# A linear-attention and bilinear-FFN kernel on one core: when chunk 1's inputs are loaded, and the orders of chunks 0 to 2

## The chip, the core and the metric

The kernel runs on one core of a Trainium2 chip. The time is the device time of one execution in microseconds (us); with one core, the slowest core is that core. A few executions are timed, and the median is given. One further execution is profiled; its span (first to last instruction) is a little shorter than its time.

The engines of the core work side by side, each through its own queue in order: TensorE (PE; its weight loads are listed as PEld), VectorE (DVE), ScalarE (ACT), GpSimd (POOL) and SyncE (SP, which here only issues transfers).

## The reference

Two stages, one after the other. First a recurrent linear attention with a gate per row of the state, for 4 batch rows, 8 heads, 768 steps and head size 48:

```python
for t in range(S):
    state = alpha[:, :, t, :, None] * state + np.einsum('bhd,bhe->bhde', k[:, :, t], v[:, :, t])
    y[:, :, t] = np.einsum('bhd,bhde->bhe', q[:, :, t], state)
```

Then a feed-forward layer on the 3,072 tokens of 384 features, with 1,536 hidden columns:

```python
a = x @ w_a
b = x @ w_b
return (a * b @ w_out).astype(np.float32)
```

All inputs and the output are float32. The kernel casts the weights and most operands of its matmuls to bf16.

## The kernel before

**Tiling.** The 768 steps are cut in three blocks of 256, and the batch in two pairs of rows: six chunks, numbered 0 to 5. Chunks 0 and 1 are the first 256 steps of rows 0 and 1, and of rows 2 and 3; the state is zero there. The 256 steps of a chunk lie on 128 partitions as pairs of consecutive steps. A chunk has two batch rows, called u = 0 and 1 below, and 512 tokens for the feed-forward layer.

**Stages of a chunk.** Load alpha, k, q, v (`ld`, L411); logarithm of alpha on ScalarE (`ln`, L418); prefix sums of the logarithms by matmuls with a triangular matrix (`B` L460, `A2` L510, `AQ` L505, with the even half's subtraction `Bs` L465 in chunk 0); exponentials of the sums, with both signs (`E`, L539); products of q and k with these (`mq`, `mk`, L550), for the first step of each pair also with alpha or its inverse (`lv`, L524); transposes by TensorE into PSUM and copies out of it (`C` L591, `Ce` L597 or L599), or by DMA in later chunks (`T`, L602); scores (`D`, L672), their causal mask (`M` on VectorE, L677; or `Mc` on ScalarE, L681, and `Mm` in place on VectorE, L685); state products (`K`, `KA`, L625) and the two state updates (`k`, L657, L660, L661), with decays from TensorE (`dk` L571, `de` L576) or by way of DRAM (`dr` L556, `dl` L561); the products of queries with carried states (`SA`, `SB`, L696 or L701) and of masked scores with v (`Y`, L696 or L722); the eviction of the result as xT (`X`, L762 or L764).

Then the feed-forward layer: hidden columns go in 12 blocks of 128. Block f of the gate (`a`) and of the up product (`b`) are three matmuls each (L784), over 512 tokens or, for one u alone, over 256. The gate is copied out by ScalarE (`as`, L790), and VectorE multiplies copy and up product (`pr`, L798). Output rows are four tiles of 128 tokens per chunk, each 12 matmuls in two halves (`o`, L806), evicted (`ot`, L821 or L823) and stored (`st`, L839).

**Weights.** `W a` and `W b` load columns of the two hidden weights and `Wo` blocks of the output weights, all issued by GpSimd (L391, L394). Each comes in pieces: columns 0 to 256, 256 to 768, 768 to 1,536.

**What sets the order.** The kernel is written with a manual schedule. A string, `PROGRAM` (L17 to L265), lists the operations chunk by chunk in one sequence, and a loop at the end (L927) records them in that order. Each engine then works through its own operations in the string's order, and waits only where data or a buffer are not ready; an operation of one engine that stands late in the string does not hold up another engine's. So a transfer is issued by its queue's engine (P is GpSimd, Y is SyncE, V VectorE, S ScalarE) after that engine's operations that stand ahead of it in the string. PSUM has 8 banks; the last number of many operations is the bank that they take, and a bank is free again once its reader is done. One buffer for v as bf16 (`vx`), two for the scaled q and k (`QKp`), and three for the gate copies (`as_`) are shared by the chunks.

The constants are part of the string: `c1`, `cz`, `cs` clear tiles, `fill` runs matmuls on zeros, `cm 0` and `cm 1` make the two halves of the mask on GpSimd (L363 to L367), `c2`, `c3` cast the triangular matrix (L354, L357).

In the first 60 us the string of before issues on GpSimd, after chunk 0's second-row inputs: the first up weights, the mask's second half, v, the casts, the first gate weights, chunk 1's alpha of row 1, the gate and up weights to 768, chunk 1's alpha of row 0, the gate and up weights to 1,536, then chunk 1's q and k, the output weights between the inputs of chunks 1 and 2, and so on.

Of the kernel before, what the change touches and what calls it, by code (L numbers as in the profile page):

```python
# [26 lines left out]
1: ld q 0 P; ln 1  # L27
0: b 0 0 4; a 0 0 2; as 0 0; pr 0 0; D 1 0 6; D 1 1 0; M 1 1
1: ld k 0 P; l2 1 P; ld v 0 P; ld k 1 P
0: Mc 1 0; Mm 1 0 V  # L30
1: H 1 S
0: SB 1 1; a 2 0 3; a 5 0 6; a 3 0 7; as 3 0; a 4 0 4; as 4 0; as 5 0; b 4 0 0; b 3 0 7
1: L 1 V
0: pr 4 0; pr 3 0; SA 1; Y 1; X 1 V; b 2 0 0
1: A2 1 7; ld q 1 P
0: Wo 0 6
2: ld a * P
0: K 1 1 5
# [36 lines left out]
1: Y 0; D 1 1 0; SA 0; X 0 S; Mc 1 1
0: o 3 1 -; ot 3 S
1: a 2 0 4
0: o 0 1 -
1: as 2 0; b 2 0 5
2: lx V; R 0; R 1; ra 1; lv 1 q P  # L80
3: ld q * P
2: AQ 3; E 0 b; E 1 b
0: ot 0 S
2: E 1 i; E 0 i
1: D 1 0 1; pr 2 0; M 1 0; a 11 0 0
0: o 1 0 7
2: ra 0
1: as 11 0
2: dr; dl
1: Mm 1 1 V; v 1 V  # L90
0: st 3 Y; o 1 1 -; ot 1 V
1: a 7 0 3; b 11 0 1; pr 11 0; KA 1 64; k 1 0 V; k 1 1 V; b 10 0 5; a 10 0 7; as 10 0; a 0 0 6
2: lv 0 k V
1: pr 10 0; b 0 0 1; a 3 0 4; as 0 0; pr 0 0
# [36 lines left out]
1: o 2 1 -; ot 2 S
0: st 2 Y
1: st 2 Y
2: D 0 0 5; Mc 0 0; Mm 0 0 V; SB 0 1; SA 1; Y 1; X 1 S; XT 1
1: a 4 1 7
4: ln *
1: as 4 1; b 9 1 0; pr 9 1; o 0 0 5
3: AQ 3
2: SA 0; Y 0; X 0 S; XT 0
5: ld a * Y  # L140
1: o 0 1 -; ot 0 V; a 1 1 6; a 10 1 1; as 1 1; as 10 1
3: E 0 b; E 0 i
1: b 4 1 2; pr 4 1; b 8 1 5; b 1 1 1; a 8 1 6; b 10 1 0; pr 1 1; o 3 0 2; pr 10 1; as 8 1; pr 8 1; o 3 1 -; ot 3 S; st 3 Y
2: a 4 * 7; as 4 *
3: E 1 b
2: a 5 * 6; b 4 * 3
3: E 1 i
1: st 0 Y
3: dr
4: lx V; R 0  # L150
3: mk 0 V; mq 0 V; T 0
4: ld q * Y
2: a 1 * 2; b 5 * 0; as 5 *; pr 5 *
4: ra 1
2: b 7 * 4; b 10 * 1; pr 4 *; a 10 * 6; as 10 *; pr 10 *
# [12 lines left out]
2: a 11 * 5; as 11 *; pr 11 *
1: o 1 1 -; ot 1 S
2: a 6 * 5; as 6 *; a 8 * 3; as 8 *  # L170
3: SB 0 6; D 0 1 0; M 0 1; T 1
4: ld k * Y
3: D 1 0 4; Mc 1 0
2: b 6 * 2; pr 6 *; b 8 * 3; pr 8 *
4: R 1
3: Mm 1 0 V
4: lv 1 q V
3: SB 1 4; D 1 1 0; Mc 1 1; Mm 1 1 V; SA 0; Y 0; X 0 S; XT 0
2: o 0 0 2
4: lv 1 k V; lv 0 k V  # L180
2: o 0 1 -
4: AQ 6; E 0 i
2: ot 0 S
4: E 0 b
3: SA 1; Y 1; X 1 V; XT 1
5: ld k * Y
4: E 1 i; E 1 b; mk 1 V
5: lv 1 k P
2: o 2 0 1; o 2 1 -; o 3 0 6; o 1 0 0; o 3 1 -; o 1 1 -
4: dr  # L190
1: st 1 Y
3: a 11 * 5
2: ot 2 V; ot 3 V
# [29 lines left out]
3: pr 10 *
4: SA 1; SA 0; Y 0; X 0 S; XT 0
3: o 2 0 7; o 1 0 1
4: Mm 1 0 V
# [28 lines left out]
4: ot 1 V; o 3 0 1; o 3 1 -; ot 3 V; o 0 0 4; o 0 1 -
3: st 3 Y
5: a 3 * 7; as 3 *; b 0 * 1; b 3 * 3; a 0 * 5; as 0 *; pr 0 *; pr 3 *
# [705 lines left out]
```

## Time and profile before

| | |
|---|---|
| timed runs, median of 3 | 196.4 us (195.39 to 196.49) |
| profiled execution, time | 195.32 us |
| profiled execution, span | 193.5 us |
| bytes read from HBM, written | 25.98 MB, 4.74 MB |
| VectorE, ScalarE, GpSimd busy | 138.4, 103.3, 50.8 us |

On the page, TensorE's busy time counts modelled ends of pipelined matmuls, so neighbours overlap: the distance from the start of a group to the start of the next tells what it costs. The costliest groups are the gate and up matmuls (L784), 57.0 and 56.1 us, and the output matmuls (L806), 48.5 us. In the timelines a row is a group of equal instructions: start, time from its start to its last end, engine, line, operation, what it writes and reads, sizes, count, and in brackets the idle time of the engine before it with what ended that. In the chain of waits a row has start and length, and the engine and line that the end of the program hung on in that stretch.

### The profile page before, as it was taken

The numbers are of one execution on the slowest core, as the hardware profiler recorded it, in microseconds if no ns is written. First come the engines' busy times: TensorE is split into PE (matmuls) and PEld (weight loads), VectorE is DVE, ScalarE is ACT, GpSimd is POOL, SyncE is SP. The second block draws the span as 40 slices with busy tenths as digits, with TensorE's granted clock in tenths as the row PEclk, the third lists the DMA queues.
The fourth block names the chain that finished last, engine by engine and source line by source line (L and its number), as shares of the span: only waits on it lengthen the run. The fifth ranks groups of instructions, "written<-read, shape, count | busy, mean of one in ns | idle before, by whom it ended". The sixth has DMA issues, their size and how long they took to land.

```text
span 193.5 us, 5877 instructions
## 1 busy us (share of the span) xinstructions
PE 184.7 (95%) x2509; PEld 111.4 (58%) x2509; DVE 138.4 (71%) x230; ACT 103.3 (53%) x189; POOL 50.8 (26%) x71
## 2 busy tenths in 40 slices
PE   7889699999999998999999999999999999999993
PEld 3467475666687865744556644555544566544462
DVE  4688777999899799597979499875854871156520
ACT  4565575886775676556565235875255622154401
POOL 8999645850640425000400020050000000000000
PEclk9999999999999999999999999999999999999999
DMA  5999999999999999489995488999297005021013
GB/s 139 261 214 211 243 247 251 252 246 260 243 220 231 198 234 219 57 233 213 172 219 69 100 203 178 118 191 120 59 180 160 3 3 122 0 99 67 0 42 122
DMA packets 67162, 30.96 MB, mean 160 GB/s; under 512 B 58064, under 2 KB 65120, under 8 KB 67136
## 3 DMA queue, kind: packets, MB, share of 16 engines
q0 software_dynamic: 18640, 14.16, 41.3%
q1 hardware_dynamic: 48352, 16.34, 39.9%
q8 instruction: 19, 0.31, 0.7%
q10 hardware_dynamic: 144, 0.10, 0.2%
q14 instruction: 7, 0.06, 0.1%
HBM read 25.98 MB, written 4.74 MB: 159 GB/s over the span
## 4 chain that ended last, share of the span: by engine, by line
PE 84%; POOL 6%; DMA 5%; issue 2%; DVE 1%; ACT 0%; POOLq 0%; DVEq 0%
PE psum L784 47%; PE psum L806 24%; DMA wb_t<-in_moe_w_b_dram 5%; PE psum L672 3%; PE psum L722 2%; PE psum L625 2%; PE psum L696 2%; PE psum L701 1%; PE psum L505 1%; PE psum L817 1%; POOL v_t L411 1%; POOL a_t L411 1%; PE psum L591 1%; POOL wa_t L391 1%; DVE prod L798 1%
## 5 line engine op out<-in xcount | busy, mean ns | idle before, releaser
L784 PE MATMUL psum<-xT,wb_t 128*128 128x512 bf16 (+1 forms) x270 | 57.0, 337 | 1.3 <-DMA wb_t<-in_moe_w_b_dram 1.3
L784 PE MATMUL psum<-xT,wa_t 128*128 128x512 bf16 (+1 forms) x270 | 56.1, 337 | 0.0
L806 PE MATMUL psum<-wo_t,prod 128*128 128x384 bf16 x276 | 48.5, 326 | 0.0
L784 PEld LDWEIGHTS <-wb_t 128*128 128x128 bf16 x270 | 25.5, 98 | 21.9 <-DMA wb_t<-in_moe_w_b_dram 1.6
L784 PEld LDWEIGHTS <-wa_t 128*128 128x128 bf16 x270 | 25.6, 98 | 19.7 <-issue 0.2
L806 PEld LDWEIGHTS <-prod 128*128 128x128 bf16 x276 | 26.1, 98 | 17.0
L681 ACT ACTIVATE m<-psum 128x1024 bf16<-128x1024 f32 x16 | 16.3, 1023 | 6.1 <-PE psum L672 5.9
L823 DVE COPY ot<-psum 128x384 f32<-128x384 f32 (+1 forms) x13 | 6.9, 538 | 15.7 <-PE psum L806 13.2
L524 POOL TENSOR_TENSOR q_t<-q_t,ra 128x384 f32<-128x384 f32 x8 | 8.8, 1103 | 34.7 <-DVE prod L798 18.4
L821 ACT ACTIVATE ot<-psum 128x384 f32<-128x384 f32 (+1 forms) x12 | 5.7, 477 | 12.9 <-PE psum L806 11.9
L524 POOL TENSOR_TENSOR k_t<-k_t,a_t 128x384 f32<-128x384 f32 x5 | 6.0, 1197 | 22.8 <-DVE QKp L550 17.9
L685 DVE TENSOR_TENSOR m<-m,mask 128x1024 bf16<-128x1024 bf16 x16 | 11.6, 734 | 0.3 <-ACT m L681 0.2
L418 ACT ACTIVATE la<-a_t 128x1536 f32<-128x1536 f32 (+2 forms) x9 | 9.5, 1053 | 3.7 <-DMA a_t<-in_alpha_dram 3.7
L550 DVE TENSOR_TENSOR QKp<-k_t,invb 128x768 bf16<-128x768 f32 x10 | 11.0, 1105 | 0.2
L677 DVE TENSOR_TENSOR m<-psum,mask 128x1024 bf16<-128x1024 f32 x8 | 9.8, 1219 | 1.6 <-PE psum L672 1.5
L550 DVE TENSOR_TENSOR QKp<-q_t,beta 128x768 bf16<-128x768 f32 x10 | 9.3, 947 | 0.0
L672 PE MATMUL psum<-kqT 64*64 64x128 bf16 x384 | 8.6, 218 | 0.2 <-DVE kqT L599 0.2
L411 POOL DMA_DIRECT2D v_t<-in_v_dram x8 | 8.6, 1075 | 0.6 <-PE psum L784 0.5
L762 ACT ACTIVATE ys<-psum 128x768 bf16<-128x768 f32 x7 | 5.6, 808 | 5.6 <-PE psum L722 3.3
L672 PEld LDWEIGHTS <-kqT 64*64 64x64 bf16 x384 | 6.3, 107 | 2.7 <-issue 2.3
L411 POOL DMA_DIRECT2D a_t<-in_alpha_dram x6 | 6.3, 1043 | 5.6 <-DVE prod L798 2.9
L444 PE MATMUL psum<-wz 128*128 128x512 bf16 x17 | 5.5, 473 | 1.2 <-DVE og L336 1.2
(272 smaller groups left out, 272.0 us busy)
## 6 DMA issues: line engine op xcount, KB each, us to landing
out_dram<-ot SPq DMA_DIRECT2D x23, 192.0 KB, 2.6
a_t<-in_alpha_dram POOLq DMA_DIRECT2D x3, 768.0 KB, 14.2
k_t<-in_k_dram SPq DMA_DIRECT2D x3, 768.0 KB, 6.7
q_t<-in_q_dram POOLq DMA_DIRECT2D x2, 768.0 KB, 12.8
v_t<-in_v_dram POOLq DMA_DIRECT2D x4, 384.0 KB, 9.2
q_t<-in_q_dram SPq DMA_DIRECT2D x2, 768.0 KB, 6.7
a_t<-in_alpha_dram POOLq DMA_DIRECT2D x3, 384.0 KB, 5.7
q_t<-in_q_dram POOLq DMA_DIRECT2D x3, 384.0 KB, 13.1
```

Source lines behind the costliest of these rows:

```text
L411: eng.dma_start(out=t[:, us, hs].rearrange("p b h r d -> p (b h) (r d)"), in_=src[ch.b0 + us.start:ch.b0 + us.stop, hs, ch.s * 2 * C:(ch.s ...
L418: nc.scalar.activation(out=ch.la[:, us, hs].rearrange("p b h r d -> p (b h r d)"), in_=ch.a[:, us, hs].rearrange("p b h r d -> p (b h r d) ...
L524: eng.tensor_mul(x, x, by)
L550: eng.tensor_mul(QKp[ch.c % 2][:, u, j, :, hs, :D], src[:, u, hs].rearrange("p h r d -> p r h d"), f)
L672: nc.tensor.matmul(s2[g * HC:(g + 1) * HC, r, p, rk, :], lhsT=ch.kqT[u][rs, 1, rk, 2 * h + p, g * HC:(g + 1) * HC], rhs=queriesT(ch, u, 2 ...
L677: nc.vector.tensor_mul(m.rearrange("p r a k s -> p (r a) (k s)"), ch.s2[u, h].rearrange("p r a k s -> p (r a) (k s)"), maskn(4))
L681: nc.scalar.activation(out=m.rearrange("p r a k s -> p (r a) (k s)"), in_=ch.s2[u, h].rearrange("p r a k s -> p (r a) (k s)"), func=AF.Copy)
L685: eng.tensor_mul(x, x, maskn(4))
L784: nc.tensor.matmul(p, lhsT=(wa_t, wb_t)[w][:, kk, f * 128:(f + 1) * 128], rhs=ch.xT[:, us.start // 2:us.stop // 2, kk].rearrange("p u g s ...
L806: nc.tensor.matmul(op, lhsT=ch.prod[:, f, at:at + C], rhs=wo_t[:, f, :], start=(f == 0), stop=(f == NFF - 1))
L821: nc.scalar.activation(out=o_, in_=i_, func=AF.Copy)
L823: eng.tensor_copy(o_, i_)
```

## The change

Only `PROGRAM` is new. The set of operations is the same but for their engines, buffers and tokens per operation; the functions that they call are the same.

- Loads. Chunk 0's rows come in the same order on SyncE. On GpSimd the first gate weights and both alpha pieces of chunk 1 now stand ahead of the first up weights; the gate and up weights to column 768 follow; then chunk 1's k and q of row 0, q of row 1 and v of row 0, and only then the gate weights from 768, chunk 1's k of row 1, and the up weights from 768. Chunk 2's alpha, chunk 1's v of row 1, chunk 2's q and k, and chunk 3's alpha follow, and after them both halves of the output weights.
- Chunk 0. The product of decays of row 0 stands ahead of the transposes; the second half of the mask is made after the loads down to chunk 1's alpha of row 1; all four score tiles are masked by VectorE out of PSUM (before: two of them by ScalarE's copy and a masking in place). Gate and up products of blocks 0 to 5 run for one row at a time, blocks 6 to 11 for both.
- Chunk 1 runs its gate and up products for one row at a time before chunk 0's output matmuls start, which now follow all but a few of them.
- Three products `lv` go from GpSimd to VectorE, two casts of v from VectorE to ScalarE; one more copy of transposes and one more eviction are VectorE's.
- Chunks 3 to 5 keep TensorE's order.

The start of the string before and after:

```diff
-0: c1a; c1; fill 7 2; cz 0 q V; cz 0 b P; cs 0 m P; ci; cz 1 q V; cz 0 v V; ld a 0b Y; ln 0b; cs 0 0 P; cm 0; cu; cu2 P; B 0b 3; Bs 0b; cs 1 m P; ld v 0 P; ld a 1 P
-0: cz 1 b P; ld a 0a Y; ln 0a; B 0a 1; Bs 0a; E 0a b; fill 9 2; cus; ld q 0a Y; mq 0a V; E 0b i; ld q 0b Y; ld k 0a Y; ld k 0b Y; mk 0b V; E 0b b; mq 0b V
-0: C 0 1 5; E 0a i; mk 0a V; Ce 0 1 V; C 0 0 3; Ce 0 0 V; dk 0 6; fill 1 1; v 0 S; de 0; K 0 0 7; k 0 0 V; ln 1; cs 1 0 P; ld q 1 P; ld k 1 P; W b 0 256
-0: cm 1; ld v 1 P; c2 P; c3 P; D 0 1 5; M 0 1; D 0 0 0; SB 0 6; B 1a 4; Bs 1a; Mc 0 0; Mm 0 0 V; B 1b 5; Bs 1b; E 1a i; E 1a b; mq 1a V; mk 1a V; K 0 1 4; E 1b i
-0: v 1 V; mk 1b V; E 1b b; mq 1b V; SA 0; Y 0; X 0 S; dk 1 0; C 1 0 3; Ce 1 0 V; k 0 1 V; b 1 0 6; W a 0 256; de 1; K 1 0 5; k 1 0 V
-1: ld a 1 P
-0: W a 256 768; W b 256 768
-1: ld a 0 P
-0: W a 768 1536; C 1 1 1; a 1 0 2; as 1 0; pr 1 0; Ce 1 1 V; W b 768 1536
-1: ld q 0 P; ln 1
...
+0: c1a; c1; cz 0 b P; ld a 0b Y; cs 0 m P; fill 7 2; cz 0 q V; ci; ld a 0a Y; cz 1 q V; ld q 0a Y; cs 0 0 P; cz 0 v V; ld q 0b Y; cm 0; ld k 0a Y; ld k 0b Y; ln 0b; cu; ln 0a
+0: cu2 P; cs 1 m P; B 0b 3; ld v 0 P; B 0a 1; Bs 0b; ld a 1 P; fill 9 2; Bs 0a; cus; E 0a b; cz 1 b P; cs 1 0 P; E 0b i; mq 0a V; ld q 1 P; E 0b b; E 0a i; mk 0b V; dk 0 6
+0: c2 P; mq 0b V; c3 P; C 0 1 5; ld k 1 P; mk 0a V; v 0 S; Ce 0 1 V; C 0 0 3; ld v 1 P; de 0; K 0 0 4; Ce 0 0 S; D 0 1 0; k 0 0 V; W a 0 256; fill 1 5; ln 1; SB 0 5
+1: ld a 1 P
+0: D 0 0 2; B 1a 4; cm 1; M 0 1; M 0 0; B 1b 0; Bs 1a; K 0 1 2; Bs 1b; E 1a b
+1: ld a 0 P
+0: SA 0; Y 0; E 1a i; mq 1a V; E 1b i; W b 0 256; mk 1a V; E 1b b; mk 1b V; X 0 S; dk 1 3; W a 256 768; v 1 S; mq 1b V; C 1 0 0; k 0 1 V; C 1 1 5; W b 256 768; de 1; K 1 0 6
+0: Ce 1 1 V
+1: ld k 0 P
+0: Ce 1 0 V
+1: ln 1; ld q 0 P
+0: D 1 1 2; k 1 0 V; M 1 1
+1: ld q 1 P; ln 0
+0: SB 1 0; D 1 0 4; a 0 0 6
+1: l2 1 P
+0: a 1 0 7; M 1 0; as 0 0; b 1 0 3
...
+0: W a 768 1536
+1: H 0 S
+0: pr 0 0; X 1 S
+1: A2 1 7; L 0 V; ld k 1 P
+0: a 1 1 5; pr 1 0
+1: A2 0 1
+0: W b 768 1536; a 2 1 0
...
+0: a 10 * 4; pr 5 1
+1: lv 1 k P
+0: pr 3 1
+1: SB 0 6
+0: as 10 *; a 8 * 3
+3: ld a * P
+1: mk 1 V
+0: as 7 *; a 11 * 4
+1: Mm 0 0 V; C 1 1 1
+0: Wo 6 12; as 11 *
+1: Mm 0 1 V; C 1 0 5; Ce 1 1 S
+0: b 7 * 0; Wo 0 6
...
+2: dl; D 1 0 5; D 1 1 2; KA * 70; Mc 1 0; M 1 1
+0: o 1 1 -
+2: k * 0 V
+0: o 2 0 1; ot 1 S; st 1 Y
+2: D 0 0 4
+0: st 3 Y
+2: D 0 1 2
+4: ld a * Y
+2: M 0 0
+0: o 2 1 -
+2: Mc 0 1; Mm 1 0 V; SB 1 6
+0: ot 2 S
+2: SB 0 2
```

More of the change, by code (lines that the diff above doesn't have):

```diff
@@ L63 @@
+1: mk 0 V
+0: b 0 1 6; a 3 0 0; pr 5 0; a 4 0 4
+1: lv 0 q P
+0: as 3 0; pr 0 1; a 4 1 3; as 5 1; pr 3 0; a 3 1 0; as 4 1
+2: ld q * P
+0: b 4 0 6
+1: mq 0 V
+0: as 4 0; b 4 1 5
+1: E 1 b; C 0 1 1
+0: pr 4 1
+2: ld k * P
+1: C 0 0 4
+0: as 3 1
+1: Ce 0 1 V; v 0 S; dk * 3; Ce 0 0 V; lv 1 q P; D 0 1 1; de *; KA 0 07
+0: pr 4 0
+1: Mc 0 1
+0: K 1 1 5
+1: D 0 0 3; k 0 0 V
+0: k 1 1 V; b 5 1 6
+1: Mc 0 0
+0: b 3 1 0
+1: mq 1 V
+0: a 6 * 2; a 7 * 5
+1: k 0 1 V
+0: a 10 * 4; pr 5 1
 1: lv 1 k P
+0: pr 3 1
@@ new lines @@
+2: lv 1 q P
+1: pr 1 0; a 9 0 1; k 1 0 V; a 0 0 5; pr 2 0; as 9 0
+3: ld q * P
+1: b 0 0 0
+2: R 0; ra 0
+1: as 0 0; SB 1 5; a 6 0 1; b 3 0 2
+2: lv 0 q V; ld v * P
+1: as 6 0; b 6 0 7; pr 0 0; a 3 0 1
+2: R 1
+1: b 9 0 3; as 3 0; Y 1
+3: ln *
+1: pr 9 0; pr 6 0; SA 1
+2: AQ 0
+1: pr 3 0
+2: lv 0 k V
+1: X 1 S
+0: a 9 * 7
+2: E 1 b
+3: lx V
+0: b 9 * 2; as 9 *
+1: a 4 1 5
+2: E 1 i
+1: a 11 1 6; k 1 1 V
+2: E 0 b
+1: a 6 1 7; b 9 1 3
+2: dr
+0: pr 9 *
+1: as 6 1
+2: E 0 i
+1: b 6 1 1; a 9 1 7; as 11 1; pr 6 1; a 3 1 2; as 9 1
@@ L78 @@
+2: mq 1 V
+1: a 5 1 6; as 4 1; b 1 1 7; b 11 1 5; pr 9 1; a 0 1 1; pr 11 1; b 8 1 3; as 0 1
+2: mk 1 V
+1: a 8 1 4; b 0 1 1; as 8 1; a 2 1 5; pr 0 1
+2: T 1
+0: o 3 0 4
+3: R 0
+1: as 5 1; a 1 1 6
+2: mq 0 V
+0: o 3 1 -
+1: pr 8 1; b 2 1 0
+2: mk 0 V
+1: as 3 1; b 5 1 3
+3: ra 0
+0: o 0 0 2; ot 3 S
+3: R 1; lv 0 q P
+2: T 0
+1: b 4 1 4
 0: o 0 1 -
[L79 to L82, printed above, removed]
+1: pr 4 1; pr 5 1; as 2 1
+3: ld k * P
+0: o 1 0 4
+1: as 1 1; pr 2 1
@@ new lines @@
+1: b 3 1 5
+3: lv 0 k P
+1: as 7 1; b 7 1 1; pr 3 1; a 10 1 4
+2: k * 1 V; Y 1
+1: as 10 1
+2: Y 0
+3: ld v * P; lv 1 k V
+2: SA 1; SA 0
+3: AQ 4
+2: X 1 S; X 0 V
+5: ld a * P
+3: ra 1
+1: o 0 0 0
+2: XT 1
+3: E 0 b; E 0 i; mq 0 V
+1: o 2 0 6
+3: E 1 i
+2: XT 0
+4: ln *
+3: lv 1 q V
+1: o 2 1 -
+3: mk 0 V
+1: o 0 1 -
+4: ra 1
+1: b 10 1 7; ot 0 S; o 3 0 2; pr 10 1
+3: E 1 b
+1: st 0 Y; pr 7 1
+3: dr
+1: ot 2 V
+2: a 4 * 3; a 5 * 6; b 4 * 0; as 5 *; a 1 * 5; as 4 *
+1: o 3 1 -
+2: pr 4 *
+3: T 0
@@ L132 @@
+2: b 5 * 3
+1: ot 3 V
+2: b 10 * 0; pr 5 *; b 7 * 1
+4: lx V
+2: a 10 * 6
+0: st 0 Y
+2: a 7 * 3
+1: st 3 Y
+2: as 10 *
 0: st 2 Y
+4: R 0
+2: b 1 * 2; as 1 *
 1: st 2 Y
[L134 to L143, printed above, removed]
@@ L175 @@
+3: M 0 0
+4: lv 0 q P; ld k * Y
+2: b 11 * 0
+4: ld v * P
+3: k * 0 V
+2: a 11 * 5
+1: o 1 1 -
+3: k * 1 V
+2: as 11 *; a 6 * 5
+1: ot 1 S
+2: pr 11 *; a 8 * 3; as 6 *
+3: SB 0 6
+2: as 8 *
+3: D 0 1 0; D 1 0 4; M 0 1
+2: b 6 * 2
+3: Mc 1 0
+2: b 8 * 3; pr 6 *
+3: SB 1 4; D 1 1 0
+2: pr 8 *
+3: SA 0; Y 0; Mc 1 1
 4: R 1
-3: Mm 1 0 V
+2: o 0 0 2
+3: X 0 S; Mm 1 0 V; XT 0
+2: o 0 1 -
 4: lv 1 q V
[L178 to L181, printed above, removed]
@@ L222 @@
+4: D 0 1 5; D 0 0 3; k * 0 V
+3: b 1 * 7
+4: Mc 0 0
+3: a 3 * 0
+5: ld q * Y
+3: pr 1 *
+5: ra 0
+3: b 4 * 3
+4: Mc 0 1
+3: a 2 * 4; pr 4 *
+5: ra 1
+3: b 2 * 7; as 2 *
+4: Mm 0 0 V; gatet 1
+5: ld v * P
+3: a 7 * 1; as 3 *
+4: Mm 0 1 V
+3: a 10 * 2; pr 2 *; as 7 *
+4: SB 0 3; SB 1 5
+3: as 10 *
+4: D 1 1 0
+3: b 3 * 7
+4: Mc 1 1
+3: b 10 * 2; pr 3 *
+4: D 1 0 0; Mm 1 1 V
 5: lv 1 q P
[L223 to L226, printed above, removed]
+4: SA 1; SA 0; Mc 1 0; Y 0
+3: pr 10 *; o 2 0 7
@@ L252 @@
-5: XT 1; X 0 S
+3: o 0 1 -; ot 1 V
+4: a 7 * 0
+5: mk 0 V
+3: ot 0 S
+4: b 1 * 4; as 7 *
+5: mq 1 V
+4: b 7 * 5
+5: mq 0 V
+4: a 10 * 3
+5: T 1
+4: a 1 * 1; as 10 *; a 6 * 6; as 1 *; b 10 * 2
+5: T 0
+4: a 0 * 0; pr 10 *; b 0 * 1; pr 7 *; as 0 *; a 2 * 2; pr 1 *; as 6 *; b 6 * 7; pr 0 *; as 2 *
+5: dl
+4: b 5 * 0; pr 6 *; a 5 * 3
+3: st 1 Y
+4: b 2 * 7
+3: st 2 Y
+4: as 5 *
+3: st 0 Y
+4: a 3 * 5; pr 2 *; a 4 * 2; as 3 *; pr 5 *; a 11 * 7; as 4 *
+5: D 0 0 0
+4: as 11 *
+5: D 1 1 3
+4: b 4 * 6
@@ L253 @@
+5: Mc 0 0
+4: b 3 * 5; pr 4 *
+5: Mc 1 1
+3: o 3 0 7
+4: pr 3 *
+5: Mm 0 0 V; D 1 0 0; D 0 1 2; K * 0 5; M 1 0; Mc 0 1
+4: a 9 * 6
+5: k * 0 V
+4: b 9 * 4; as 9 *; b 8 * 0
+5: Mm 1 1 V; SB 0 2; SB 1 5; Mm 0 1 V
+4: a 8 * 1
+3: o 3 1 -
+4: as 8 *; pr 8 *; b 11 * 1
+5: Y 1
+4: pr 11 *
+5: Y 0
+4: pr 9 *
+5: SA 0; SA 1
+4: o 1 0 1
 3: ot 3 V
+5: X 1 S; X 0 S; XT 1
+4: o 1 1 -
 5: XT 0
[L255 removed]
+4: o 2 0 0; ot 1 V; o 2 1 -
 3: st 3 Y
[L257 removed]
```

292 lines of the change are left out of this document (117 added, 175 removed).

## The prediction

> **What bounds the kernel now.** I read the page's busy shares and its 40 slices first, then the windows, then the chain of waits in order of time, then the timelines of TensorE, GpSimd and VectorE.
>
> ```profile
> PE 184.7 (95%) x2509; PEld 111.4 (58%) x2509; DVE 138.4 (71%) x230; ACT 103.3 (53%) x189; POOL 50.8 (26%) x71
> ...
> PEclk9999999999999999999999999999999999999999
> DMA  5999999999999999489995488999297005021013
> ...
> q8 instruction: 19, 0.31, 0.7%
> ```
>
> TensorE is busy for 95% of a span of 193.5 us at an undiminished clock, so the time is TensorE's work plus its holes. Transfers are dense up to about slice 16 and thin out later.
>
> ```profile
> 24.00:43.00 19.00, 18.88 (x288) 12.62 (x286) 16.19 (x29) 13.79 (x28) 12.17 (x12) 1.00 1.21 248
> 43.00:62.00 19.00, 19.00 (x307) 13.73 (x304) 17.95 (x32) 12.39 (x25) 5.41 (x5) 1.00 1.20 240
> ```
>
> In these two windows (columns: TensorE, its weight loads, VectorE, ScalarE, GpSimd, clock, DMA share, GB/s) TensorE is full, and VectorE is busy 16.19 and then 17.95 of 19.00 us: it is the next limit.
>
> ```profile
> 14.38 8.97 DMA wb_t<-in_moe_w_b_dram
> ...
> 67.61 0.54 PE psum L625 x64
> 68.15 1.09 PE psum L784 x9
> 69.24 0.97 PE psum L806 x6
> 70.21 0.24 PE psum L701 x16
> 70.45 0.23 PE psum L672 x16
> 70.69 1.08 PE psum L806 x6
> 71.77 0.35 PE psum L672 x16
> 72.11 0.12 PE psum L701 x16
> 72.23 1.26 issue
> ```
>
> The chain goes through a weight transfer up to 23.35 us, then almost only through TensorE. One hole in the middle has no releaser: 1.26 us of "issue" at 72.23, in chunk 2, after a run of small matmuls.
>
> ```profile
> 23.40 0.83 PE L784 MATMUL psum<-xT,wb_t 128*128 128x256 bf16 x6 [1.30 <-DMA wb_t<-in_moe_w_b_dram]
> ...
> 25.37 0.42 PE L510 MATMUL psum<-lh,utr 128*128 128x384 f32 x1
> ...
> 36.02 0.72 PE L591 MATMUL psum<-ident,QKp 128*128 128x128 bf16 x8
> ...
> 36.98 0.49 PE L784 MATMUL psum<-xT,wb_t 128*128 128x256 bf16 x3
> 37.59 0.44 PE L625 MATMUL psum<-vx,QKp 64*64 64x48 bf16 x32
> ...
> 38.42 0.49 PE L784 MATMUL psum<-xT,wb_t 128*128 128x256 bf16 x3
> ```
>
> Two holes lie in the part that the change lays out anew: 1.30 us for the up weights at 23.40, and a looser one from 36.02 to 38.42, where chunk 1's inputs have just come. Those 2.40 us hold 16 transposes (8 take 36.57 - 36.02 = 0.55), 6 matmuls of 256 columns (0.109 each: 3 take 0.33) and 32 small ones (37.96 - 37.59 would be 0.37): 1.10 + 0.65 + 0.1 to 0.37, so some 0.3 to 0.55 is lost. I take 0.5, because the small matmuls stand at about 0.01 each at 67.61.
>
> **The change, part by part.** Both programs have the same matmuls, 2,469 in the built order, and the same fills; nothing is saved in work. From chunk 3's state products on, TensorE's order is the same. So the sum is made of holes, against the profiled execution: 195.3 us, of which the span is 193.5. The three timed runs before have a median of 196.4, 1.1 above it; I carry that 1.1.
>
> *The head: the mask.* GpSimd makes the second half of the mask and issues most transfers, in one queue.
>
> ```profile
> 6.60 0.89 POOL L411 DMA_DIRECT2D q_t<-in_q_dram  x1
> ...
> 9.16 0.31 POOL L363 MEMSET mask<- 64x256 bf16 x1
> ...
> 10.24 0.24 POOL L367 TENSOR_SCALAR_AFFINE_SELECT mask<-mask 64x64 bf16<-64x64 bf16 x1
> 10.56 0.90 POOL L411 DMA_DIRECT2D v_t<-in_v_dram  x1
> 11.51 0.28 POOL L354 CAST utr<-ut 128x128 fp32r<-128x128 f32 x1
> ...
> 11.99 0.76 POOL L391 DMA_DIRECT2D wa_t<-in_moe_w_a_dram  x1
> 12.74 0.92 POOL L411 DMA_DIRECT2D a_t<-in_alpha_dram  x1
> ```
>
> Before, the mask is done at 10.24 + 0.24 = 10.48. After the change there stand between q_t (done 7.49) and the mask: two casts (11.99 - 11.51 = 0.48), k_t (0.9), v_t (0.95), wa_t (0.75), chunk 1's a_t (0.92), then the four steps of the mask (1.3): done at 12.8. The first masking waits for it.
>
> ```profile
> 11.72 1.21 DVE L677 TENSOR_TENSOR m<-psum,mask 128x1024 bf16<-128x1024 f32 x1
> ...
> 14.04 0.36 DVE L465 TENSOR_TENSOR psum<-psum,la 128x192 f32<-128x192 f32 x1
> 14.47 0.56 DVE L550 TENSOR_TENSOR QKp<-q_t,prod 128x384 bf16<-128x384 f32 x1
> ...
> 16.94 0.55 DVE L550 TENSOR_TENSOR QKp<-q_t,prod 128x384 bf16<-128x384 f32 x1
> ```
>
> It moves from 11.72 to 12.85, and now two full maskings (1.2 each) stand ahead of the even half sums that L465 gives for the second batch row, where before one stood there with a cheaper masking in place. So the last L465 ends at about 15.8, not 14.4. Its four exponentials and products follow: the last product ends near 17.8, against 17.49, since before it had waits of its own. Queued behind it on VectorE are the copies of the transposes, three state steps and the next two maskings; I count them to 22.6. The inner matmuls then end near 23.1 and the prefix sums (L510) start at 23.65.
>
> Before, L510 starts at 25.37, but with 33 gate and up matmuls behind it; after, the order has 12 of them by then. The 21 missing ones cost 21 x 0.109 = 2.3: 23.65 + 2.3 = 25.95, which is 0.6 late although the wait of 1.30 is gone. Chunk 0's next matmul needs the second row's xT, whose copy ScalarE ends at about 24.4: another 0.3. Term: **+0.9** (bounds: -1.3, if the mask costs nothing and the weight wait alone goes; +2.2, VectorE's whole hole from 10.6 to 12.8). The product of decays that now runs ahead of the transposes sits in a hole of TensorE of about 0.8 and costs nothing; without that hole it is 0.5.
>
> *The transfers.* The up weights of columns 256 to 768 stand behind one more a_t piece (384 KB, at 248 GB/s 1.6 us): near 24 to 25, needed at 26. The last gate and up weights, 11.2 and 13.3 us on their way before:
>
> ```profile
> wa_t<-in_moe_w_a_dram POOLq DMA_DIRECT2D x1, 576.0 KB, 11.2
> wb_t<-in_moe_w_b_dram POOLq DMA_DIRECT2D x1, 576.0 KB, 13.3
> ```
>
> They were issued at 16.0 and 16.8 and landed at 27.2 and 30.1. With k, two q and a v piece (1.34 MB, 5.4 us) ahead, and one more k piece ahead of the second, they land near 32.6 and 37.1. TensorE asks for them at about 34.5 and 38.7, after chunk 0's 24 half products on the first 768 columns. Output weights, last, land about 10 us later than before, near 55; their first use moves from 43 to 60. So no wait, with 1.5 to 2 us of cover; each us beyond it is a us lost. The hole at 36 to 38 goes, as chunk 1's first inputs come some 5 us earlier: **-0.5** (0 to -0.6).
>
> *VectorE from 24 to 62.* The change moves onto it three products of q or k with alpha, one copy of transposes and one eviction, and makes two maskings full; it loses two casts of v: about +3.4 us in all.
>
> ```profile
> 36.20 0.72 DVE L798 TENSOR_TENSOR prod<-as__705,psum 128x512 bf16<-128x512 bf16 x1
> 36.82 0.71 DVE L798 TENSOR_TENSOR prod<-as__716,psum 128x512 bf16<-128x512 bf16 x1
> 37.43 0.43 DVE L798 TENSOR_TENSOR prod<-as__710,psum 128x256 bf16<-128x256 bf16 x1
> 37.76 0.43 DVE L798 TENSOR_TENSOR prod<-as__741,psum 128x256 bf16<-128x256 bf16 x1
> ```
>
> From start to start a product takes 0.62 or 0.33. From the first masking of chunk 0's second row to chunk 0's first output matmul the new order has 6 and 28 of these (13.0 us) and 22 us of other work: 35 us, beside 38.4 us of TensorE's. That is 91%; the windows show 85% and 94% kept up without TensorE waiting much. I take **0** (bounds -0.3 and +3.5).
>
> *The issue hole.* From 67.61 to 72.23 there are 149 matmuls, each with its weight load. After the change the same place (state products, two output halves, 32 scores, an output half, 32 carried products) has 146, priced from the same rows 0.54 + 1.95 + 0.58 + 0.97 + 0.36 = 4.4 us against 4.62. If the hole comes from instructions arriving too slowly, it becomes 1.26 + 0.2: **+0.2** (bounds -1.26 and +1.5, a second such hole).
>
> The page of queues has 19 packets of 0.31 MB for instructions, 264 of the 5,018 records to a packet. [...]
>
> Sum: 0.9 - 0.5 + 0 + 0.2 = +0.6: 195.9 on the profiled execution's scale, 197.0 on the median's. I say 196.9.
>
> **Rivals.**
> 1. *VectorE becomes the bound (slower).* No output matmuls, which ask nothing of VectorE, lie any more between 43 and 60, so each burst on it (1.1 for a masking, 0.87 for a product of k) is met by TensorE waiting for a PSUM bank. VectorE has 38.4 us for its 35, so it decides once it is kept below 91% busy. At the first window's 85% it needs 35 / 0.85 = 41.2 us: 2.8 more than the forecast, 199.7. For it: 94% from 43 to 62. Against: that stretch lost nearly nothing.
> 2. *The mask is hidden and the issue hole goes (faster).* If the maskings have slack, the head gains 0.5 instead of losing 0.9, and the hole of 1.26 belongs to something that the new order lacks: 196.4 - 0.5 - 0.5 - 1.26 = 194.1. For it: the first inner products end 2 us earlier. Against: the in-order queue of VectorE. [...]
> 3. *A weight piece comes late (slower too).* 2 us beyond its cover: 198.9. For it: DMA is full until 60. Against: the two margins above.
>
> That the change does nothing is excluded by the order lists.
>
> **How the numbers follow.** Within 1% (194.4 to 198.4; the runs before spread over 0.6%, so less can't be told): the forecast, 0.43. Slower by more: rival 1 at 0.25 and rival 3 or a second issue hole at 0.10, so 0.35. Faster by more: rival 2, 0.22. The range is 194.0 to 200.0: it takes in rival 2's value and rival 1's, and leaves out some 0.2 beyond them; the forecast's own range is 195.2 to 198.4.
>
> **What would show it.** First masking of VectorE at 12.8, not 11.7; no wait on wb_t near 23; L510 first at about 23.7; no hole near 36; a hole of "issue" in chunk 2 of 1 to 2 us; VectorE above 90% busy from 43 to 60. It is wrong if TensorE waits on a DMA between 25 and 60, if its waits on VectorE there sum to over 2 us, or if the issue hole is missing.

## The result, and the profile after

The changed kernel takes 206.5 us in the median of four runs (205.22 to 208.23), before takes 196.1 beside it: a ratio of 1.054, with a 95% interval of 1.046 to 1.063. It is slower by 5%, outside the range forecast. Ratios, here and below, leave out executions that fell in the chip's slower state, and medians don't. The profiled execution of the changed kernel has a span of 203.4 us, 9.9 more than before.

The page of the changed kernel, busy shares and slices:

```profile
span 203.4 us, 5870 instructions
...
PE 187.0 (92%) x2509; PEld 113.3 (56%) x2509; DVE 140.1 (69%) x233; ACT 101.3 (50%) x187; POOL 48.4 (24%) x69
...
PE   7877998998999957969999899999999999999993
...
PEclk9999999999999995899999999999999999999998
```

TensorE has the same matmuls and 2.3 us more busy time; its busy share dips to 5 tenths in slice 15, and its clock falls in the two slices behind that. The other 7.6 us are holes. Where do they lie? From chunk 3's state products on TensorE's order is the same in both kernels, so the start of these 64 matmuls is a milestone. Timeline of TensorE, before and then after:

```profile
94.25 0.69 PE L625 MATMUL psum<-v_t,QKp 64*64 64x48 bf16 x64
```

```profile
103.24 0.70 PE L788 MATMUL psum<-v_t,QKp 64*64 64x48 bf16 x64
```

Of the 9.9 us, 9.0 are lost by this point. The larger holes between 25 us and this point, in the timeline of the changed kernel (start, time, what runs, and in brackets the idle time before it):

```profile
29.82 0.82 PE L947 MATMUL psum<-xT,wa_t 128*128 128x256 bf16 x6 [0.41 <-DVE prod L961]
...
32.14 0.84 PE L754 MATMUL psum<-ident,QKp 128*128 128x128 bf16 x12 [0.62 <-DVE QKp L713]
...
48.98 1.80 PE L947 MATMUL psum<-xT,wb_t 128*128 128x256 bf16 x15 [0.89 <-DVE prod L961]
...
76.96 0.20 PE L864 MATMUL psum<-Sm,kqT 64*64 64x48 bf16 x1 [3.21 <-DVE Sm L824]
...
78.09 0.80 PE L947 MATMUL psum<-xT,wa_t 128*128 128x256 bf16 x3 [0.51 <-DVE m L840]
...
90.52 1.45 PE L947 MATMUL psum<-xT,wa_t 128*128 128x512 bf16 x6 [1.86 <-DMA xT<-ys]
```

There are two groups: three waits for VectorE from 29 to 49 us, 1.92 in all, and a stage from 73.6 to 90.5 with 5.6 us of waits. That stage hangs on transfers. Its chain of waits (start, length, what the end hung on):

```profile
65.94 1.67 POOL q_t L687
67.61 0.01 issue
67.62 1.15 SPq L724
68.77 0.06 issue
68.83 7.01 DMA bl<-row
...
75.97 0.06 DVE Sm L824
76.03 0.80 issue
76.83 1.22 DVE m L840
78.05 0.04 issue
78.09 2.72 PE psum L947 x12
80.81 1.40 PE psum L885 x64
...
85.79 4.68 DMA xT<-ys
```

(The product of GpSimd in the first row only happened to end last ahead of the load's issue: SyncE's own waits from 58 to 70 us name ScalarE, VectorE and TensorE, and not GpSimd, and SyncE issued the load 0.2 us after its second transpose.) The state of chunk 2 (`Sm`) needs the decays `bl`, which SyncE loads from DRAM (`dl`, L724). That load is issued in two halves up to 68.83, and lands 7.01 us later. VectorE stands still behind it from 71 to 76, and the masking queued next on it ends at 78.05. Two more numbers are in these rows. The 12 matmuls at 78.09 take 2.72, where 0.109 each makes 1.31, and the 64 inner products behind them 1.40, where before does 32 in 0.51, from 73.74 to 74.25: 1.8 us go to a slow clock. The windows show it (columns as in the prediction):

```profile
74.00:76.00 2.00, 0.00 (x0) 0.00 (x0) 0.03 (x1) 0.27 (x1) 0.50 (x1) 0.99 1.09 287
76.00:82.00 6.00, 4.54 (x108) 3.44 (x107) 5.16 (x8) 0.77 (x2) 1.64 (x2) 0.50 1.18 159
```

TensorE stopped for 3.2 us, and for the next 6 us its granted clock was 0.50. So the stage costs 5.6 of waits and 1.8 of clock, where before loses 1.26.

Why the decays were late is in SyncE's queue. Before:

```profile
50.65 1.32 SPq L556 DMA_DIRECT2D row<-beta  x2
56.59 0.92 SPq L561 DMA_DIRECT2D bl<-row  x2
...
60.15 6.08 SPq L602 DMA_TRANSPOSE kqT<-QKp  x2
66.40 0.52 SPq L411 DMA_DIRECT2D k_t<-in_k_dram  x1
...
75.19 5.18 SPq L769 DMA_TRANSPOSE xT<-ys  x2
80.56 0.45 SPq L411 DMA_DIRECT2D a_t<-in_alpha_dram  x1
```

After:

```profile
58.74 1.32 SPq L719 DMA_DIRECT2D row<-beta  x2
62.51 4.93 SPq L765 DMA_TRANSPOSE kqT<-QKp  x2
67.62 1.91 SPq L724 DMA_DIRECT2D bl<-row  x2
```

And GpSimd's queue after:

```profile
67.55 1.21 POOL L574 DMA_DIRECT2D k_t<-in_k_dram  x1
...
82.25 1.17 POOL L574 DMA_DIRECT2D a_t<-in_alpha_dram  x1 [4.61 <-DVE k_t L687]
```

In the old order `dl` stood right behind `dr`. In the new one it stands some 30 lines later, behind both transposes by DMA, and the second of these waits for VectorE's last product of k. Chunk 3's load of k, which SyncE issued before, now comes from GpSimd at 67.55, 768 KB, a moment ahead of the small load. And chunk 5's load of alpha, which stood on SyncE behind both transposes of xT, is now GpSimd's and stands ahead of them in the string: it is issued at 82.25, the transposes from 83.44 on. These three moves are in the diff and in the order lists. So are two more: chunk 3's load of v now stands behind a product of GpSimd that waits for chunk 3's k (issued at 76.44, before at 67.58), and chunk 4's load of alpha, 768 KB, went from GpSimd at 55.83 to SyncE at 72.62. The prediction has no term for any of them.

### The profile page after: what moved, and what is told of

Same layout as the page of the kernel before. It is cut to its first block, busy times and chain, and to the rows that moved or that the text cites. A ratio compares the mean times of both kernels' runs of the same rounds, so it can differ in the third digit from the quotient of the medians.

```text
span 203.4 us, 5870 instructions
## 1 busy us (share of the span) xinstructions
PE 187.0 (92%) x2509; PEld 113.3 (56%) x2509; DVE 140.1 (69%) x233; ACT 101.3 (50%) x187; POOL 48.4 (24%) x69
## 4 chain that ended last, share of the span: by engine, by line
PE 56%; DMA 23%; POOL 10%; issue 7%; DVE 1%; SPq 1%; ACT 0%; POOLq 0%; DVEq 0%; ACTq 0%
PE psum L947 32%; PE psum L969 16%; DMA k_t<-in_k_dram 9%; DMA q_t<-in_q_dram 8%; DMA bl<-row 3%; DMA xT<-ys 2%; PE psum L885 2%; POOL q_t L687 2%; PE psum L835 2%; POOL a_t L574 1%; PE psum L864 1%; POOL q_t L574 1%; PE psum L980 1%; POOL v_t L574 1%; PE psum L788 1%
## 5 line engine op out<-in xcount | busy, mean ns | idle before, releaser
L844 ACT ACTIVATE m<-psum 128x1024 bf16<-128x1024 f32 x14 | 14.1, 1022 | 4.9 <-PE psum L835 4.8
L687 POOL TENSOR_TENSOR q_t<-q_t,ra 128x384 f32<-128x384 f32 x6 | 6.8, 1127 | 35.1 <-DMA q_t<-in_q_dram 20.1
L840 DVE TENSOR_TENSOR m<-psum,mask 128x1024 bf16<-128x1024 f32 x10 | 12.0, 1218 | 3.4 <-PE psum L835 1.8
L687 POOL TENSOR_TENSOR k_t<-k_t,a_t 128x384 f32<-128x384 f32 x4 | 4.5, 1120 | 37.7 <-DMA k_t<-in_k_dram 37.7
L713 DVE TENSOR_TENSOR QKp<-q_t,beta 128x768 bf16<-128x768 f32 x10 | 10.2, 1031 | 0.5 <-ACT beta L702 0.5
L835 PE MATMUL psum<-kqT 64*64 64x128 bf16 x384 | 9.6, 219 | 0.3 <-DVE kqT L762 0.3
L713 DVE TENSOR_TENSOR QKp<-k_t,invb 128x768 bf16<-128x768 f32 x10 | 9.5, 951 | 0.1
L848 DVE TENSOR_TENSOR m<-m,mask 128x1024 bf16<-128x1024 bf16 x14 | 9.2, 683 | 0.0
L925 ACT ACTIVATE ys<-psum 128x768 bf16<-128x768 f32 x6 | 4.7, 808 | 5.2 <-PE psum L864 3.6
L864 PE MATMUL psum<-Sm,kqT 64*64 64x48 bf16 x128 | 4.2, 197 | 3.2 <-DVE Sm L824 3.2
```

What stands on the lines that cost most here:

```text
L687: eng.tensor_mul(x, x, by)
L713: eng.tensor_mul(QKp[ch.c % 2][:, u, j, :, hs, :D], src[:, u, hs].rearrange("p h r d -> p r h d"), f)
L835: nc.tensor.matmul(s2[g * HC:(g + 1) * HC, r, p, rk, :], lhsT=ch.kqT[u][rs, 1, rk, 2 * h + p, g * HC:(g + 1) * HC], rhs=queriesT(ch, u, 2 ...
L840: nc.vector.tensor_mul(m.rearrange("p r a k s -> p (r a) (k s)"), ch.s2[u, h].rearrange("p r a k s -> p (r a) (k s)"), maskn(4))
L844: nc.scalar.activation(out=m.rearrange("p r a k s -> p (r a) (k s)"), in_=ch.s2[u, h].rearrange("p r a k s -> p (r a) (k s)"), func=AF.Copy)
L848: eng.tensor_mul(x, x, maskn(4))
```

## The experiments

The numbers give the order in which they ran. Ratios are to before on the same chip, with 95% intervals; medians stand beside them. The ratios are what is compared; one per cent is 1.95 us.

**1. The decays alone.** The changed kernel with `dl` where before has it:

```diff
-2: dr
+2: dr; dl
...
-2: dl; D 1 0 5; D 1 1 2; KA * 70; Mc 1 0; M 1 1
+2: D 1 0 5; D 1 1 2; KA * 70; Mc 1 0; M 1 1
```

> After, with chunk 2's decay load (dl) put back right behind the store of the decays (dr), ahead of both transposes by DMA; nothing else. Theory A (the load of the decays stands in SyncE's queue behind the transposes of u = 0, and lands at 75.4 us): the decays land by about 65, TensorE's hole of 3.2 us at 73.6, the half clock from 76 to 82.5 and the wait of 1.9 for xT at 90.5 go. Behind the kernel before stay the 2.6 us lost by 60 us and a hole of instruction supply of 1 to 2 us: 197 to 199.5. Theory B (VectorE is the bound, the late decays only hide it): VectorE's queue still holds up the maskings near 73 to 77, and the time stays at 203 or above.

Measured: 206.5 us (203.59 to 207.89), ratio 1.047 (1.040 to 1.054). The load was issued at 61.99 and the hole at 73.6 is gone, and yet little is won. TensorE's timeline:

```profile
75.34 0.50 PE L947 MATMUL psum<-xT,wa_t 128*128 128x256 bf16 x3 [0.47 <-DVE m L848]
...
81.27 2.77 PE L969 MATMUL psum<-wo_t,prod 128*128 128x384 bf16 x16 [1.24 <-issue]
...
88.95 2.72 PE L947 MATMUL psum<-xT,wa_t 128*128 128x512 bf16 x6 [3.61 <-DMA xT<-ys]
```

It ran into the next wait sooner: 3.61 us for xT, and 1.24 of issue. Neither theory held as it was put. Some of the loss in this profiled execution is of the head and not of this stage: the clock was 0.57 from 20 to 24 us, where the changed kernel's was 1.00, and TensorE's first gate matmuls for the second row's xT start at 25.64, not at 24.18. The transposes of xT (SyncE's timeline) and the load issued beside them (GpSimd's):

```profile
78.87 3.29 SPq L932 DMA_TRANSPOSE xT<-ys  x2
```

```profile
76.80 1.20 POOL L574 DMA_DIRECT2D v_t<-in_v_dram  x1
78.89 1.17 POOL L574 DMA_DIRECT2D a_t<-in_alpha_dram  x1 [0.89 <-DVE k_t L687]
```

In its chain of waits the second transpose counts for 8.54 us, from 80.37 to 88.91. The load of alpha, 768 KB, took 9.4 to land.

**2. The load beside the decays.** Decays left late, chunk 3's k issued by SyncE behind them:

```diff
-3: ld k * P
...
-2: dl; D 1 0 5; D 1 1 2; KA * 70; Mc 1 0; M 1 1
+2: dl
+3: ld k * Y
+2: D 1 0 5; D 1 1 2; KA * 70; Mc 1 0; M 1 1
```

> After, with chunk 3's k load taken from GpSimd and issued on SyncE right behind chunk 2's decay load; the decay load itself stays behind the transposes. Theory A with contention (the small decay load took 6.6 us to land because a k load of 768 KB was issued 0.1 us ahead of its first half): it lands some 2.7 us after its issue, near 71.5, the product Sm by 72.4 instead of 76.9, the hole at 73.6 shrinks to under 0.8, the clock stays full: 198 to 201. If only the place in the queue matters: as after, 204 to 207.

Measured: 205.9 us, 1.051 (1.043 to 1.059). TensorE's timeline:

```profile
74.11 0.18 PE L865 MATMUL psum<-Sm,kqT 64*64 64x48 bf16 x1 [0.26 <-DVE Sm L825]
...
88.93 2.74 PE L948 MATMUL psum<-xT,wa_t 128*128 128x512 bf16 x6 [4.60 <-DMA xT<-ys]
```

The mechanism shows, the time doesn't: `Sm` starts at 73.50 and not at 75.97, and of the hole of 3.21 only 0.26 is left. The load of k did hold the decays up, by about 2.5 us, though they still took some 4.6 us and not the 2.7 expected; and the next late transfer, xT, took what that gave.

**3. The same fault put into before.**

```diff
-2: dr; dl
+2: dr
...
 2: T 0
 3: ld k * Y
+2: dl
```

> Before, with chunk 2's decay load alone moved behind the transposes of u = 0 and chunk 3's k load, all on SyncE. Theory A: the load is issued near 67 instead of 56.6 and lands near 73 to 75, VectorE's product with it waits from 69.2, TensorE stops for 2 to 5 us in the place of the issue hole and its clock falls: 199 to 205. Theory B: the place of this load is worth nothing: 195 to 197.

Measured: 202.0 us, 1.034 (1.030 to 1.037), with nothing else changed. Chain of waits, then TensorE's timeline:

```profile
68.57 6.75 DMA bl<-row
```

```profile
76.05 0.19 PE L702 MATMUL psum<-Sm,kqT 64*64 64x48 bf16 x1 [5.45 <-DVE Sm L662]
```

Theory A held, with a stop a little longer than it said. The place of this one small load is worth 6.6 us in the old order.

**4. The mask, on top of the early decays.** The mask's second half is made ahead of v's load of the second row:

```diff
-...; ld v 1 P; de 0; K 0 0 4; ...
+...; cm 1; ld v 1 P; de 0; K 0 0 4; ...
...
-0: D 0 0 2; B 1a 4; cm 1; M 0 1; M 0 0; ...
+0: D 0 0 2; B 1a 4; M 0 1; M 0 0; ...
```

> The first experiment's kernel with the mask's second half also made 2.7 us earlier, ahead of the load of v for the second pair of rows, near where before has it. If the late mask cost the head what the prediction put there (0.9, of which the first masking's 1.1 us of delay is the cause): 0.5 to 1.2 below the first experiment. If VectorE's later work takes it back, or the mask's delay was hidden: within 0.4 of it.

Measured: 201.0 us, 1.028 (1.022 to 1.033): 0.019 below the first, 3.7 us, well over what was expected. The slow clock of the first run's head may be a part of this; the seventh run has the mask without it.

**5. The alpha load, on top of the early decays.**

```diff
-5: ld a * P
...
 2: XT 0
+5: ld a * Y
```

> The first experiment's kernel, with chunk 5's alpha load (768 KB) put back on SyncE behind chunk 2's second xT transpose, as before has it; after the change it is issued on GpSimd at 78.9 us, in the same 0.02 us as the first transpose. Theory C (with the decays early, the next late thing is xT: the two transposes were issued at 78.9 and 80.4 and landed at 88.9, beside this load, which landed at 88.3): xT lands 2 to 5 us earlier, TensorE's wait of 3.6 us at 88.9 falls under 1, its clock stays full after it, and the time is 199 to 203. Rival (the transposes are slow by themselves, or beside other loads): no change, 203 to 207.

Measured: 200.1 us, 1.024 (1.020 to 1.028), 4.4 us below the first by the ratios. The wait for xT falls from 3.61 to 1.52, not under 1. In the chain its transfer is shorter, but not short:

```profile
79.75 6.27 DMA xT<-ys
```

**6. All three.**

> All three: decays early, mask early, chunk 5's alpha load behind the transposes. The fourth run was even with before in priced work by 60 us and by 80 us, and lost 4.0 us in the wait for xT plus some 1.5 at a lower clock behind it. If these three places are the whole loss: 194 to 197, level with before. If something else is late behind xT: 198 to 201.

Measured: 197.5 us, 1.010 (1.005 to 1.016). TensorE reaches the milestone at 96.51. Left over in its timeline behind 60 us are 1.28 put down to a masking (which ended 0.39 before TensorE went on), 0.96 of issue and 0.87 for xT. Most of the loss was in the three places, not all.

**7. The mask alone.** The changed kernel with the mask's edit only.

> After with the mask's second half made ahead of v's load, alone. The late decays stay. If the mask's 1.9 us only moves everything after it to an earlier place, up to the wait for the decays: that wait hangs on VectorE's product mk of u = 0, which comes some 2.5 to 3.5 us earlier too: 202 to 204. If the decays' landing doesn't move with it: as after, 205 to 207.

Measured: 203.1 us (202.90 to 203.61), 1.039 (1.035 to 1.043): 3 us. First masking in VectorE's timeline, after the change:

```profile
12.79 2.36 DVE L840 TENSOR_TENSOR m<-psum,mask 128x1024 bf16<-128x1024 f32 x2 [1.56 <-POOL mask L530]
```

and in this run:

```profile
11.15 2.35 DVE L840 TENSOR_TENSOR m<-psum,mask 128x1024 bf16<-128x1024 f32 x2
```

The 1.64 us are passed on in full and grow: chunk 2's state products start at 66.28 and not at 69.33. The wait for the decays comes as much earlier, as the first theory had it: 2.91 us up to 73.60, not 3.21 up to 76.96. TensorE's waits for VectorE from 25 to 49 us are 0.35 (0.16 and 0.19) in place of 1.92. The windows from 24 us, after the change and then in this run:

```profile
24.00:43.00 19.00, 17.78 (x304) 12.98 (x306) 16.27 (x31) 12.35 (x28) 10.26 (x11) 1.00 1.20 250
43.00:62.00 19.00, 18.05 (x262) 13.86 (x252) 18.61 (x36) 13.85 (x29) 4.58 (x4) 1.00 1.04 182
```

```profile
24.00:43.00 19.00, 18.79 (x324) 13.18 (x322) 17.63 (x31) 14.08 (x28) 10.47 (x10) 1.00 1.20 248
43.00:62.00 19.00, 18.81 (x243) 14.73 (x241) 18.52 (x39) 12.46 (x29) 4.25 (x4) 1.00 1.12 204
```

VectorE is busy for 36.15 of 38 us here, 95%, more than the 34.88 of the changed kernel, and TensorE hardly waits for it. Having started late is what VectorE couldn't make good.

**8. Chunk 3's v as well**, issued ahead of GpSimd's product that waits for chunk 3's k:

```diff
-3: lv 0 k P
+3: ld v * P; lv 0 k P
...
-3: ld v * P; lv 1 k V
+3: lv 1 k V
```

> The sixth kernel with chunk 3's v load also ahead of GpSimd's product that waits for chunk 3's k, so that it is issued near 66 to 70 and not at 73.6, ahead of the transposes of xT. If the transposes are held up by whatever load lands beside them: 0.5 to 2 below the sixth. If by chunk 5's alpha load alone: within 0.5 of it.

Measured: 196.2 us, 1.006 (1.003 to 1.009), 0.9 below the sixth by the ratios, whose intervals overlap. The trace tells more than the time: there is no wait for xT any more, and the second transpose, issued at 77.4, lands at 80.2, 2.8 us later, where it took 5.71 in the sixth. So it was not one load alone that held the transposes up, but both. What is left behind 60 us:

```profile
71.89 0.50 PE L947 MATMUL psum<-xT,wa_t 128*128 128x256 bf16 x3 [0.46 <-DVE m L848]
78.36 2.77 PE L969 MATMUL psum<-wo_t,prod 128*128 128x384 bf16 x16 [1.78 <-issue]
```

**10. The alpha load alone.** The changed kernel, decays late, mask late.

> After, with chunk 5's alpha load alone put back behind the second xT transpose on SyncE; the decays stay late. In the changed kernel the wait for xT is 1.9 us at 90.5, with the alpha load landing at 89.2. If both late things cost separately: the wait for xT goes and the hole of 3.2 at 73.6 stays: 203.5 to 205. If the late decays alone bring the whole loss of this stage: as after, 205.5 to 207.

Measured: 203.2 us, 1.039 (1.036 to 1.041): 3 us, a little more than expected. The wait for xT is gone, the hole at 73.6 is there with 3.60. What a late transfer costs depends here on whether a later one covers it: the early decays are worth 1.5 us by themselves (1.054 to 1.047, intervals that overlap), and 2.8 once the alpha load is out of the way (1.039 to 1.024).

**11. The mask made late in before.**

```diff
-0: cm 1; ld v 1 P; c2 P; c3 P; D 0 1 5; ...
+0: ld v 1 P; c2 P; c3 P; W a 0 256
+1: ld a 1 P
+0: cm 1; D 0 1 5; ...
```

> Before, with the mask's second half made behind v, both casts, the first gate weights and chunk 1's alpha of row 1, so that it is done near 14 instead of 10.5, and the first masking starts 2.3 us later than its scores allow. If a late mask is passed on by VectorE's queue to everything behind it in the head, as it did in the changed kernel (1.9 us of mask, 2.6 us by 60 us): before loses 1 to 3 us, 196.5 to 198.5. If the wait of 1.3 for the up weights at 23.4 takes it up: within 0.5 of before.

Measured: 198.3 us, 1.013 (1.009 to 1.016). The wait for the up weights at 23 us is gone from its timeline, and the kernel still loses 2.4 us. The clock was at 0.50 to 0.70 of full speed from 16 to 24 us in the profiled execution, which is a part of it: the one execution of the four with a mean clock of 1.00 took 197.1 us, 1.6 above the median of before.

**9, 12 and 13. The hole of issue, in before.** Twelve output matmuls moved ahead of it:

```diff
-1: o 2 1 -; ot 2 S
+1: o 2 1 -; ot 2 S; o 0 0 5; o 0 1 -; ot 0 S
...
-2: D 0 0 5; Mc 0 0; ...
+2: D 0 0 6; Mc 0 0; ...
...
-1: a 4 1 7
+1: a 4 1 5
...
-1: as 4 1; b 9 1 0; pr 9 1; o 0 0 5
+1: as 4 1; b 9 1 0; pr 9 1
...
-1: o 0 1 -; ot 0 V; a 1 1 6; ...
+1: a 1 1 6; ...
```

> Before, with chunk 1's six + six output matmuls of tile 0 (12 x 0.163 = 1.96 us) moved from behind the hole of 1.26 us at 72.23 to ahead of the 32 small matmuls in front of it; their banks are changed to suit (the scores of u = 0, half 0, take banks 6 and 7, the gate of block 4 takes bank 5), and ScalarE evicts the tile in place of VectorE. The hole stands ahead of matmul 1118 of the trace; in the other runs holes without a releaser stand ahead of matmuls 1118, 1246 and 1630, which are multiples of 128 apart, with 128 matmuls and 128 weight loads each. Theory F (instructions come in blocks of 256, and a block of TensorE's queue that is worked off faster than the next one comes ends in a wait): with 1.96 us more work in the block the hole at 1118 is under 0.2, and the time is 1.0 to 1.3 below before, unless xT, whose first transpose is issued 0.7 later, is waited for (then 0.3 to 1.0 below). Rival (the hole belongs to the carried products that stand behind it): it moves along with them, 1.2 us long, and the time is within 0.3 of before.

Measured: 196.3 us, 1.005 (1.002 to 1.008). The hole ahead of matmul 1118 is gone, but the early eviction waited for a buffer that a store still read, and TensorE lost 1.15 and 0.80 to that, then ran at 0.57 of its clock from 78 to 82. With a fifth buffer (`bufs=5` for `ot`), and before with the fifth buffer alone as its control:

> The ninth kernel with five buffers in place of four for the evicted output tiles. In the ninth, the hole of 1.26 at matmul 1118 was gone, but ScalarE's early eviction of tile 0 waited 3.1 us, up to 76.1, for a buffer that an earlier store still read; TensorE then lost 1.15 and 0.80, at a lower clock from 78 to 82. Theory F (blocks of instructions): with the buffer the gain stays: 0.5 to 1.3 below before. If the work moved ahead of the block is missed behind it (xT, or the next block at matmul 1246): within 0.5 of before.

> Before with five buffers for the evicted output tiles, alone: the control for the run beside it. No engine of before waits long for such a buffer on the path of TensorE: within 0.3 of before under every theory.

Measured: 195.4 us, 1.001 (0.999 to 1.003), and for the control 195.8, 1.001 (0.999 to 1.004). Neither differs from before. In the first the hole is back at the next multiple, ahead of matmul 1246:

```profile
75.83 0.36 PE L505 MATMUL psum<-l,utb 64*64 64x384 bf16 x4 [0.33 <-ACT ys L762]
...
78.17 0.60 PE L784 MATMUL psum<-xT,wa_t 128*128 128x256 bf16 x4 [0.69 <-issue]
```

0.69 and 0.33 make up 1.02 of the 1.26 that went. The work that filled one block was taken out of the next: its 128 matmuls are worked off in 3.6 us from matmul 1118 to the hole, where the block ahead of the hole in before took 4.6. No version here beats before.

The traces' records of transfers bear on what comes late. They hold 19 packets of 16 KB in the queue for instructions. Ahead of each of the 17 holes without a releaser in these runs, all from 70 to 120 us, such a packet ends 1.25 to 1.68 us before TensorE goes on: in before it ends at 71.86 and TensorE goes on at 73.50, after the change at 114.41 and 115.83. That fits a block of instructions that has to arrive first, but is no more than the author's reading: no run changed how instructions are fetched.

## Why the prediction was wrong

**The step that failed** is "So the sum is made of holes" as it was carried out: the four terms count TensorE's order, VectorE, and the inputs and weights up to 60 us, and put at nothing, without a reason, what the new string does to transfers between 60 and 90 us. Missing are the load of chunk 2's decays, moved from behind their store to behind both transposes, the loads of chunk 3's k and chunk 5's alpha, moved from SyncE to GpSimd and so out of the order that kept them behind the small transfers, and chunk 3's v, now issued 9 us later. In ratios: decays and alpha load put back take 5.9 us off (1.054 to 1.024); with the mask 8.6 (to 1.010); with chunk 3's v 9.4 (to 1.006). The runs add up to a cause, and the run with the late decays in before shows one of them without the rest. Chunk 4's alpha was put back in no run; what its move costs is open, and so is the last 0.6%.

**The head (+0.9).** The mechanism and the times were right: first masking at 12.79 (12.85 forecast), prefix sums at 23.09 (23.65), no wait for up weights near 23. The size was not: the late mask alone costs 3 us by the ratios, over the term's upper bound of 2.2; in before it costs 2.4, a slow clock included. The prediction priced what TensorE is short of by 26 us and took the rest as hidden. The delay stayed in VectorE's queue and came out at 29.8, 32.1 and 49.0.

**The transfers (-0.5).** Right as far as they were counted: the last gate weights landed at 32.8 (32.6 forecast) and the last up weights at 36.6 (37.1), and TensorE waits for no weights behind 20 us. Rival 3, a late weight piece, did not happen. The hole at 36 was read a little high: at the rate of the row at 67.61, 32 small matmuls take 0.27, which leaves 0.4 lost and not 0.5; and TensorE now waits 0.62 for VectorE ahead of chunk 1's transposes, at 32.14.

**VectorE (0), and rival 1.** With the mask in time VectorE kept up at 95% busy, over the 91% below which rival 1 was to decide. The term of 0 was right for the work moved onto VectorE, and rival 1 named the engine at which TensorE waits, but not the reason. The waits on VectorE from 25 to 60 us, 1.92, stayed just under the 2 us that the prediction named as a sign against it.

**The issue hole (+0.2).** In the changed kernel a wait for data lies over its place, ahead of matmul 1086, so the term was not to be seen; the missing hole was a sign that the prediction had named against itself. Where the decays come early, a hole without a releaser stands one block later, with 0.96 to 1.78 us. That instruction supply makes it was not shown, but fits what the runs show: every such hole stands ahead of matmul 1118, 1246 or 1630, multiples of 128 apart (with a weight load to each matmul, 256 records of the trace), behind the end of a packet of instructions; with the block ahead of 1118 filled, the twelfth run has one ahead of 1246, 0.69 us. How fast a block is worked off doesn't decide alone: the block up to 1630 takes 4.1 us in before, without a hole, and 4.9 after the change, 0.63 of it a hole.

**The bounds.** 200.0 at the top came from VectorE. No rival had a small transfer behind a large one in it, so no bound did.

## What to carry to other kernels

When a schedule is laid out anew, list for each queue that issues transfers what stood ahead of each one before and what stands ahead of it now, small ones first: here a load of 3 KB on the path of a state was late by the two transposes ahead of it in its queue, and then by the 768 KB issued beside it (7.01 us to land, some 4.6 with these issued behind it). Two late transfers in a row can hide each other: putting the decays back alone gave 1.5 us here, and with the alpha load out of the way 2.8. Put both back, or put one into the old kernel. VectorE, busy for 92 to 95% of the time from 24 to 62 us, did not make good a late start of 1.64 us; for such an engine, price a wait at the start by what follows it, and not only by what is short at once.

## What the hardware showed

After a stop of 3.2 us the clock was 0.50 for 6 us (1.8 us lost). In the seventh run stops of 2.91 and 2.84 us were each followed by 0.53 to 0.61 over some 4 us, and in the ninth two waits of 1.15 and 0.80 us, 0.8 apart, by 0.57 over the next 4 us. Holes of 1.26 (before), 1.78 (eighth run) and 1.86 (the changed kernel) by themselves left it at full speed, 1.00 behind each. How long a stop has to be for the clock to fall was not shown. In some executions the clock also fell in the head, to 0.50 to 0.70 between 16 and 24 us in the eleventh run, 0.57 from 20 to 24 in the first and 0.63 and 0.52 from 18 to 22 in the sixth, in others of nearly the same kernel not (1.00 in the changed kernel and in the eighth run), which may be why the first experiment's runs spread over 4 us; that was not tested.

Small transfers took longer here with large ones beside them. The list of transfers of before has these medians (KB each, where given, and us from issue to landing):

```profile
bl<-row SPq DMA_DIRECT2D x8, 3.0 KB, 3.0
xT<-ys SPq DMA_TRANSPOSE x8, 3.1
```

Beside a load of 768 KB the decays took 7.01 and, in the third run, beside chunk 3's k and v, 6.75. The second transfer of xT took 4.68 in the chain of the changed kernel, 8.54 in the first run with two loads issued within 2.1 us of the first transpose, 6.27 in the fifth with one of these taken away, and 2.8 in the eighth with the other out of the way too.
